# One hand-written order for all work from the last batch's outputs to the third item

## The chip, the cores and the metric

The kernel runs on one core of one Trainium2 chip. The metric is the device time of one execution in microseconds (us), lower is better, given as a median of runs. Times inside the text are positions in one profiled execution, counted from the start of its span.

## The reference

Attention without softmax feeds a router that sends each of 4608 tokens to one of 8 experts; a gated layer follows.

```python
kv = np.einsum('bhsd,bhse->bhde', k, v)            # 8 batches, 8 heads, 576 rows, width 64
out = np.einsum('bhsd,bhde->bhse', q, kv)
rms = np.sqrt(np.mean(out * out, axis=-1, keepdims=True) + 1e-06)
x = out / rms * g_norm                              # -> 4608 tokens of width 512
logits = x @ w_gate + modality_bias[modality_id]
e_idx = np.argmax(logits, axis=1)                   # one expert of 8 for each token
gate_w = softmax(logits)[arange, e_idx]
for e in range(8):
    mask = e_idx == e
    h = np.maximum(x[mask] @ w1[e], 0.0)            # 512 -> 1024
    out[mask] = gate_w[mask, None] * (h @ w2[e])    # 1024 -> 512
out = (sigmoid(out @ moe2_w_gate) * (out @ moe2_w_val)) @ moe2_w_out
```

## The kernel before

The program has three stages: attention by batch, the experts by item, and the gated layer. An item is a pair of 128-token tiles of one expert. `gather` (L200) fetches a tile's rows out of the DRAM tensor `x_d` by an indirect DMA that POOL issues; `norm_x` (L230, DVE) scales it; `emit_A` (L238) transposes it on PE and splits it into a high part `xh` (ACT) and a rest `xl` (DVE). An item has four steps, j = 0 to 3. In each step `emit_B` (L251) runs 24 matmuls with a block of w1, `emit_h` (L270) takes the relu, and `emit_D` (L305) runs 12 matmuls with a block of w2, or 8 full float32 ones where `plain` says so (odd j of items 0 and 1). `split_w` (L214) splits a block of weights on ACT (`w1h`, `w2h`) and DVE (`w1l`, `w2l`).

The first two items are formed from the first four batches alone, so that their matmuls can run while the router still counts the other tokens. The third item, t = 2, needs the finished router: after the last batch's outputs (`emit_out`, L489, with a copy and a square on ACT and a reduce on DVE) come `norm`, `choose`, `rank`, `lanes`, `numbers`, then `totals`, `segments`, `slots` and `tokens`, which end in the row list `gidx`, and `experts`, which ends in the list of experts `est`. `store_x` (L588) writes a batch to `x_d`, one DMA of 1152 KB and, for odd batches, two of 144 KB. The gather of item 2 reads any row of `x_d`, so it comes after the store of batch 7 as well.

The order is the order of emission: `manual_schedule` keeps each engine's instructions, and the DMAs that it issues, in the order of the Python code. SP issues all weight loads (`load_w`, L185) and all stores of `x_d`. Items 0, 1 and 2 share one weight buffer, `half`: each block is loaded for the next item once its last reader is done, so that SP waits at such a load for a `split_w` on DVE, or for a plain `emit_D` on PE. `read_item` (L163) makes SP read `est` into registers, and SP waits there for DVE. Loads for item 2 carry a condition (`cond=new`): where item 2 has the expert of item 1, the DMA is issued and nothing is moved.

Before, all of this is in two loops. The loop over batches (L661) has one extra round, b = 8, for the outputs of batch 7; the loop over the eight steps of items 0 and 1 (L847) hangs the router's pieces on the steps by a table:

```python
CHAIN = {0: [ranks2, norm_last], 1: [lanes2, lambda: choose(3)], 2: [number(2, 0), ranks], 3: [number(2, 1), totals, lanes3, segments, number(3, 0)],
         4: [slots, number(3, 1)], 5: [tokens], 6: [experts], 7: [places]}
```

In what follows the names are those of the change's list: `out3`, `o3`, `sq3`, `ssq3` are the matmuls, copy, square and reduce of row group 3 of batch 7; `n7b` is the end of `norm(7)`; `nx21`, `A21`, `xh21`, `xl21` belong to tile 1 of item 2; `w1h6`, `w1l6`, `B6`, `h6`, `hl6`, `w2h6`, `w2l6`, `D6` belong to step 6 (item 1, j = 2), and B8 is the first step of item 2; `L2_3` loads w2's block 3 for item 1; `S7` stores batch 7; `exp` is `experts` and the two `read_item` calls; `g0` and `g1` are gathers for items 2 and 3.

Of the kernel before, what the change touches and what calls it, by code (L numbers as in the profile page):

```python
# [35 lines left out]
NFRONT = 2  # L36
# [48 lines left out]
def attention_moe_glu_kernel(  # L85
# [76 lines left out]

    def read_item(t):  # L163
# [36 lines left out]
    def gather(t):  # L200
        if t >= al.end:
            return
        for i in range(tiles_of(t)):
# [10 lines left out]
    def split_w(t, j, which):  # L214
# [10 lines left out]
        hi, lo = al.w2() if which else [w1p.tile(shape, F32R, tag=nm + z, name=nm + z, bufs=3) for z in "hl"]  # L225
        nc.scalar.activation(out=hi, in_=src, func=ACTF.Copy)
        nc.vector.tensor_tensor(out=lo, in0=src, in1=hi, op=ALU.subtract)  # L227
        dst[t, j] = (hi, lo)
# [9 lines left out]
    def emit_A(t, i):  # L238
# [6 lines left out]
        if i == 0:  # L245
            xT_t[t] = [xp.tile([128, KC, 256], F32R, tag=z, name=z) for z in ("xh", "xl")]
        hi, lo = (z[:, :, i * 128:i * 128 + 128] for z in xT_t[t])
        nc.scalar.activation(out=hi, in_=ps, func=ACTF.Copy, scale=gcol)  # L248
        nc.vector.scalar_tensor_tensor(out=lo, in0=ps, scalar=gcol, in1=hi.bitcast(F32), op0=ALU.mult, op1=ALU.subtract)  # L249
# [20 lines left out]
    def emit_h(t, j):  # L270
# [13 lines left out]
        nc.scalar.activation(out=hi[:, :, 0:n], in_=ph, func=ACTF.Relu)  # L284
        nc.vector.scalar_tensor_tensor(out=lo[:, :, 0:n], in0=ph, scalar=0.0, in1=hi[:, :, 0:n].bitcast(F32), op0=ALU.max, op1=ALU.subtract)
# [53 lines left out]
    with ExitStack() as st:  # L339
# [149 lines left out]
        def emit_out(b, r):  # L489
# [6 lines left out]
            for hp in range(4):  # L496
                for lo, n, c in ([(0, 128, b)] if r < 4 else [(0, 64, b - 1), (64, 64, b)]):
                    nc.tensor.matmul(out=ps[lo:lo + n, hp // 2, (hp % 2) * 144:(hp % 2) * 144 + 144],
                                     lhsT=qt[:, hp, lo:lo + n], rhs=Rs[c % 3][:, hp, :], start=True, stop=True)
            nc.scalar.activation(out=o[:, r, :].rearrange("p (a f) -> p a f", a=2), in_=ps[:, :, 0:288], func=ACTF.Copy)  # L500
            sq = wk.tile([128, H, D], F32, tag="sq", name="sq")
            sqv, ov = sq.rearrange("p (c s) d -> p c (s d)", s=2), o[:, r, :].rearrange("p (c f) -> p c f", c=4)[:, :, 0:128]
            nc.scalar.activation(out=sqv, in_=ov, func=ACTF.Square)
            nc.vector.tensor_reduce(out=ssq[:, 8 * t:8 * t + 8], in_=sq, op=ALU.add, axis=AX)

        def norm(b):

# [5 lines left out]
            nc.vector.tensor_scalar(out=ms, in0=ms, scalar1=1.0 / D, scalar2=1e-6, op0=ALU.mult, op1=ALU.add)  # L513
            nc.scalar.activation(out=rt[:, v], in_=ms, func=ACTF.Sqrt)
            nc.vector.reciprocal(out=rs, in_=rt[:, v])
# [26 lines left out]

        def rank(bp):

            t0, n = 9 * bp, 9
            og = oh[:, t0:t0 + n, :]
            tr = sm.tile([128, 8], F32, tag="tr", name="tr")
            nc.vector.tensor_reduce(out=tr, in_=og.rearrange("p t e -> p e t"), op=ALU.add, axis=AX)
            nc.vector.tensor_tensor(out=tot[:, bp + 1, :], in0=tot[:, bp, :], in1=tr, op=ALU.add)
# [3 lines left out]
            for i in range(1, n):  # L553
                nc.tensor.matmul(out=ps[:, i:n, :], lhsT=onesb, rhs=og[:, 0:n - i, :], start=False, stop=(i == n - 1))
            me = me_t.pop(bp)
# [4 lines left out]
            lane = sm.tile([128, 9], BF16, tag="lane", name="lane")  # L560
# [962 lines left out]
```

## Time and profile before

| | us |
|---|---|
| median of 3 runs | 1483.66 |
| lowest and highest | 1482.23, 1486.6 |
| the profiled execution | 1486.05 |
| its span | 1484.3 |
| PE busy in the span | 1433.2 (97%) |
| the changed stretch, `out0` to B8 | 131.73 to 203.80 |

A row of a timeline gives the start, the time an instruction took, engine, line, operation, what it writes and reads, and in brackets the idle time of the engine before it with what ended it. A row of the windows gives, for a stretch, its length, each engine's busy time and number of instructions, then the clock that TensorE was granted (1.00 is 2.4 GHz, 0.50 is 1.2 GHz, a value between is a mean over the stretch), the share of the DMA engines that was busy and GB/s.

### The profile page before, as it was taken

How to read it: one execution, taken by the hardware profiler on the slowest of the kernel's cores; microseconds unless marked ns; L12 is line 12 of the kernel's file. 1: busy time of each engine (PE TensorE's matmuls, PEld its weight loads, DVE VectorE, ACT ScalarE, POOL GpSimd, SP SyncE). 2: the span in 40 equal slices, each digit the busy share in tenths (PEclk: the TensorE clock that was granted, in tenths of full speed). 3: DMA queues.
4: the chain of work that ended last, by engine and by line, in shares of the span. 5: the costliest groups of instructions: out<-in, count | busy, mean ns of one | idle time of the engine just before them, and what ended most of it. 6: DMA issues, size and time to landing. Idle time of an engine off the chain costs nothing.

```text
span 1484.3 us, 22966 instructions
## 1 busy us (share of the span) xinstructions
PE 1433.2 (97%) x8654; PEld 1223.9 (82%) x8654; DVE 902.5 (61%) x1418; ACT 639.0 (43%) x1019; POOL 218.5 (15%) x302
## 2 busy tenths in 40 slices
PE   6988899999999999999999999999999999999997
PEld 6977678999999998778888888888888888888886
DVE  2557767888888888647876676343653436444342
ACT  3656645555555555746433342232322323221221
POOL 1011021212222122311011101010010200101001
PEclk9999999999999999999999999999999999999999
DMA  9976469989896856959886666556474564646444
GB/s 297 335 289 239 180 226 282 314 289 300 289 296 207 256 182 224 307 204 351 323 333 250 245 234 237 211 199 248 156 261 188 216 231 171 247 165 235 179 156 166
DMA packets 161954, 360.49 MB, mean 243 GB/s; under 512 B 20912, under 2 KB 80560, under 8 KB 154672
## 3 DMA queue, kind: packets, MB, share of 16 engines
q1 hardware_dynamic: 149904, 325.42, 63.7%
q0 software_dynamic: 10432, 32.08, 5.9%
q8 instruction: 70, 1.15, 0.3%
q10 hardware_dynamic: 1504, 1.48, 0.3%
q14 instruction: 44, 0.36, 0.1%
HBM read 302.88 MB, written 68.63 MB: 250 GB/s over the span
## 4 chain that ended last, share of the span: by engine, by line
PE 54%; DMA 4%; SPq 0%; issue 0%; DVE 0%; ACT 0%; POOL 0%; POOLq 0%; ACTq 0%
PE gv L986 10%; PE gv L988 10%; PE gv L987 10%; PE ac L1354 6%; PE ac L1352 6%; PE ac L1353 6%; DMA xg<-x_d,gidx 3%; PE gv L962 1%; PE gv L960 1%; PE gv L961 1%; PE tr L923 1%; DMA rows<-w_d 1%; DMA half<-in_moe_w_dram 0%; DMA y_d<-y,sidx 0%; SPq L1075 0%
## 5 line engine op out<-in xcount | busy, mean ns | idle before, releaser
L990 DVE TENSOR_TENSOR gm<-u,gv 128x512 f32<-128x512 f32 x96 | 65.8, 685 | 172.5 <-PE gv L988 171.3
L265 PE MATMUL ph<-xh,w1h 128*128 128x256 f32 x576 | 167.8, 291 | 2.7 <-ACT xh L248 1.7
L1354 PE MATMUL ac<-wos,gl 128*128 128x512 f32 x432 | 168.3, 389 | 0.0
L1352 PE MATMUL ac<-wos,gh 128*128 128x512 f32 x432 | 168.2, 389 | 0.0
L1353 PE MATMUL ac<-wos,gh 128*128 128x512 f32 x432 | 168.1, 389 | 0.0
L266 PE MATMUL ph<-xh,w1l 128*128 128x256 f32 x576 | 164.6, 286 | 2.7 <-DVE w1l L227 2.7
L267 PE MATMUL ph<-xl,w1h 128*128 128x256 f32 x576 | 164.5, 286 | 0.6 <-DVE xl L249 0.6
L1010 ACT ACTIVATE s<-gv 128x512 f32<-128x512 f32 x48 | 28.7, 597 | 262.4 <-issue 205.7
L265 PEld LDWEIGHTS ph<-xh,w1h 128*128 128x128 f32 x576 | 111.5, 194 | 5.7 <-ACT xh L248 2.2
L266 PEld LDWEIGHTS ph<-xh,w1l 128*128 128x128 f32 x576 | 111.6, 194 | 4.7 <-DVE w1l L227 3.3
L986 PE MATMUL gv<-half,wt 128*128 128x512 f32 x288 | 112.9, 392 | 0.7 <-DVE u L990 0.7
L267 PEld LDWEIGHTS ph<-xl,w1h 128*128 128x128 f32 x576 | 111.7, 194 | 1.0 <-DVE xl L249 1.0
L988 PE MATMUL gv<-half,wt 128*128 128x512 f32 x288 | 112.2, 390 | 0.0
L987 PE MATMUL gv<-half,wt 128*128 128x512 f32 x288 | 112.1, 389 | 0.0
L317 PE MATMUL py<-w2h,hh 128*128 128x512 f32 x272 | 106.7, 392 | 0.0
L318 PE MATMUL py<-w2l,hh 128*128 128x512 f32 x272 | 106.7, 392 | 0.0
L319 PE MATMUL py<-w2h,hl 128*128 128x512 f32 x272 | 105.9, 389 | 0.0
L990 DVE TENSOR_TENSOR s<-u,gv 128x512 f32<-128x512 f32 x48 | 33.0, 688 | 118.6 <-PE gv L988 118.5
L1336 POOL DMA_INDIRECT out_dram<-ot,to x36 | 37.0, 1027 | 435.2 <-DVE ot L1333 187.3
L1354 PEld LDWEIGHTS ac<-wos,gl 128*128 128x128 f32 x432 | 81.1, 188 | 17.3 <-DVE gl L1321 0.4
L1352 PEld LDWEIGHTS ac<-wos,gh 128*128 128x128 f32 x432 | 81.1, 188 | 16.9 <-ACT gh L1320 0.2
L1353 PEld LDWEIGHTS ac<-wos,gh 128*128 128x128 f32 x432 | 81.1, 188 | 16.9
(309 smaller groups left out, 3341.0 us busy)
## 6 DMA issues: line engine op xcount, KB each, us to landing
wt<-wt_d SPq DMA_DIRECT2D x36, 1536.0 KB
half<-in_moe_w_dram SPq DMA_DIRECT2D x96, 512.0 KB
wos<-wo_d SPq DMA_DIRECT2D x96, 512.0 KB
w1r<-in_moe_w_dram SPq DMA_DIRECT2D x40, 512.0 KB
w2r<-in_moe_w_dram SPq DMA_DIRECT2D x40, 512.0 KB
rows<-w_d SPq DMA_DIRECT2D x24, 512.0 KB
wt<-wt_d SPq DMA_DIRECT2D x48, 256.0 KB
wt_d<-wt SPq DMA_DIRECT2D x12, 1024.0 KB
```

The costliest lines, as they stand in the source:

```text
L265: nc.tensor.matmul(out=o, lhsT=bh[:, c, cs], rhs=hi[:, c, 0:n], start=(c == 0), stop=False)
L266: nc.tensor.matmul(out=o, lhsT=bl[:, c, cs], rhs=hi[:, c, 0:n], start=False, stop=False)
L267: nc.tensor.matmul(out=o, lhsT=bh[:, c, cs], rhs=lo[:, c, 0:n], start=False, stop=(c == KC - 1))
L317: nc.tensor.matmul(out=o, lhsT=hi[:, f, cs], rhs=bh[:, f, :], start=first, stop=False)
L318: nc.tensor.matmul(out=o, lhsT=hi[:, f, cs], rhs=bl[:, f, :], start=False, stop=False)
L319: nc.tensor.matmul(out=o, lhsT=lo[:, f, cs], rhs=bh[:, f, :], start=False, stop=last)
L986: nc.tensor.matmul(out=o, lhsT=wh, rhs=yh[:, c, :], start=first and c == 0, stop=False, skip_group_check=True)
L987: nc.tensor.matmul(out=o, lhsT=wh, rhs=yl[:, c, :], start=False, stop=False, skip_group_check=True)
L988: nc.tensor.matmul(out=o, lhsT=wl, rhs=yh[:, c, :], start=False, stop=last and c == 1, skip_group_check=True)
L1352: nc.tensor.matmul(out=o, lhsT=gh[:, cs], rhs=wh, start=(k == 0), stop=False)
L1353: nc.tensor.matmul(out=o, lhsT=gh[:, cs], rhs=wl, start=False, stop=False)
L1354: nc.tensor.matmul(out=o, lhsT=gl[:, cs], rhs=wh, start=False, stop=(k == NJ - 1))
```

## The change

`emit_out`, `norm`, `rank`, `totals`, `segments`, `tokens`, `places`, `split_w`, `emit_A` and `emit_h` become generators that stop between their parts on different engines. The rest of the code calls them through `whole`, which runs all parts at once. The extra round of the batch loop, the table and the loop over steps go; a list of some 190 names takes their place and is run from left to right. A load for item 2 is emitted after the first name behind `exp` at which its block's last reader has been emitted. The amount of computation stays, with one piece on another engine.

```diff
+        def whole(parts):
+            for _ in parts:
+                pass
...
-        for b in range(B + 1):
+        for b in range(B):
...
-                if b > 2 and b % 2 == 0:
-                    if r == 0 and early or r == 1 and b == 4:
-                        lane = rank(b // 2 - 2)
-                    elif r == 1 and early or r == 3 and b == 4:
-                        lo = lanes(b // 2 - 2, lane)
...
+                if (b, r) in ((4, 1), (5, 4)):
+                    rank(b - 4)
+                if (b, r) in ((4, 3), (6, 0)):
+                    lanes(b // 2 - 2)
...
+                if early and r == 1:
+                    numbers(1, nc.scalar, (0,))
+                    numbers(1, nc.vector, (1,))
...
-        for s, (t, j) in enumerate(steps):
-            emit_B(t, j)
-            emit_h(t, j)
...
+            if t == 0:
+                for w in range(2):
+                    todo[f"L{w + 1}_{j}"] = lambda j=j, w=w: load_w(1, j, w)
...
+        place(ch3=lambda: choose(3), slots=slots, plx=exps, y0=lambda: emit_y(0), y1=lambda: emit_y(1),
+              g0=lambda: gather(NFRONT, (0,)), g1=lambda: (gather(NFRONT, (1,)), gather(NFRONT + 1)),
+              exp=lambda: (experts(), read_item(NFRONT), read_item(NFRONT + 1)))
+        behind = [(f"w1l{NJ1 + j}", j, 0) for j in range(NJ1)] + [(("D" if plain(1, j) else "w2l") + str(NJ1 + j), j, 1) for j in range(NJ1)]
+        ORDER = """
+            w1h1 out0 nx01 out1 w2h0 w1h2 o1 nx00 A00 xh00 nx10 A01 n6a w2l0 o0 xl00 nx11 out2 xh01 w1h0 xl01 out3 w1l0 rk2p o3
+            sq0 rk2 n6s o2 A11 xh11 B0 L2_0 A10 w2h2 w1l1 w1l2 sq1 ssq0 w1h3 ssq1 h0 S5 ln2 out4 sq2 hl0 o4 B1 ssq2 L1_0 w1l3 sq3
+            L1_2 h1 w1h4 B2 sq4 D0 xh10 h2 L1_1 n6b nu2b S6 xl11 xl10 nu2a B3 w2l2 ssq4 ssq3 D1 w1l4 n7a n7s hl2 B4 n7b w2h4 w1h5
+            w1h6 ch3 h4 w1l5 rk3p w1l6 rk3 D2 w2l4 ln3 h3 L1_3 nu3a B5 hl4 totp D3 tot sega segb slots soh B6 D4 exp nu3b php w1h7
+            plx gidx w1l7 h5 plc L2_2 h6 L2_1 D5 L2_3 w2h6 B7 w2l6 S7 g0 hl6 g1 nx20 A20 D6 h7 pld w1h8 nx21 xh20 A21 xl20 w1l8
+            xh21 D7 xl21 y0 y1
+        """.split()
+        done = set()
+        al.end = NSURE
+        for name in ORDER:
+            todo[name]()
+            done.add(name)
+            if "exp" in done:
+                for job in [x for x in behind if x[0] in done]:
+                    load_w(NFRONT, *job[1:])
+                    behind.remove(job)
```

The queue of SP before, from the store of batch 7 to the read of `est`; `half` rows are weight loads, the last three of them w2's blocks 2, 1 and 3 for item 1:

```order
L590 DMA x_d<-o 128x2304 [waits DMAHW2_49,Pool_49]
L594 DMA x_d<-o 64x576 [waits DMAHW3_49]
L594 DMA x_d<-o 64x576 [waits DMAHW4_49]
...
L189 DMA half_1812<-in_moe_w_dram 128x2x512 [waits DMAHW7_49,DVE_49]
L189 DMA half_1812<-in_moe_w_dram 128x2x512 [waits DMAHW0_49,PE_49]
L189 DMA half_1812<-in_moe_w_dram 128x2x512 [waits DMAHW1_49,PE_49]
L169 TENSOR_LOAD est [waits DVE_49]
```

The same queue now, from the read of `est` to the store of batch 7; between the two stand five loads for item 2, then w2's blocks 2 and 1 for item 1, block 1 for item 2 (it waits for D5 on PE), block 3 for item 1 and block 2 for item 2 (it waits for `w2l6` on DVE):

```order
L173 TENSOR_LOAD est [waits DVE_49]
...
L193 DMA half_1804<-in_moe_w_dram 128x2x512
L193 DMA half_1804<-in_moe_w_dram 128x2x512 [waits DMAHW2_49,PE_49]
L193 DMA half_1804<-in_moe_w_dram 128x2x512 [waits DMAHW2_49,PE_49]
L193 DMA half_1804<-in_moe_w_dram 128x2x512 [waits DMAHW4_49]
L193 DMA half_1804<-in_moe_w_dram 128x2x512 [waits DMAHW5_49,DMAHW1_49,DVE_49]
L623 DMA x_d<-o 128x2304 [waits DMAHW6_49,Pool_49]
L627 DMA x_d<-o 64x576 [waits DMAHW7_49]
```

Three loads for item 1 and the store of batch 7 have moved from ahead of the read of `est` to behind it, and the store also behind a load that waits for D5.

PE before, from D5 (`py<-half,hf`) by B7 (`ph`) and D6 (`py<-w,...`) to the transposes of item 2 (`xtp`):

```order
L315 MATMUL py<-half_1812,hf 128x512 x4
L265 MATMUL ph<-xh,w1h 128x256
L266 MATMUL ph<-xh,w1l 128x256
L267 MATMUL ph<-xl,w1h 128x256
...
L317 MATMUL py<-w_2512,hh 128x512
L318 MATMUL py<-w_2512,hh 128x512
L319 MATMUL py<-w_2512,hl 128x512
...
L244 MATMUL xtp<-ident,xg 128x128 x4
L315 MATMUL py<-half_1812,hf 128x512 x4
L244 MATMUL xtp<-ident,xg 128x128 x4
```

PE now, from D5 again:

```order
L332 MATMUL py<-half_1804,hf 128x512 x4
L278 MATMUL ph<-xh,w1h 128x256
L279 MATMUL ph<-xh,w1l 128x256
L280 MATMUL ph<-xl,w1h 128x256
...
L255 MATMUL xtp<-ident,xg 128x128 x4
L334 MATMUL py<-w_2548,hh 128x512
L335 MATMUL py<-w_2548,hh 128x512
L336 MATMUL py<-w_2548,hl 128x512
...
L255 MATMUL xtp<-ident,xg 128x128 x4
L332 MATMUL py<-half_1804,hf 128x512 x4
```

The two transposes of item 2 have each moved ahead by one `emit_D`: A20 stands ahead of D6, and A21 ahead of D7.

## Rows read from the trace of the kernel before

**Rows 1.** The page: busy time and share by engine; below, PE's busy tenths by slice.

```profile
PE 1433.2 (97%) x8654; PEld 1223.9 (82%) x8654; DVE 902.5 (61%) x1418; ACT 639.0 (43%) x1019; POOL 218.5 (15%) x302
PE   6988899999999999999999999999999999999997
```

**Rows 2.** Windows: busy time by engine, granted clock, DMA share, GB/s.

```profile
131.70:203.80 72.10, 62.57 (x445) 49.51 (x445) 53.33 (x137) 40.15 (x80) 6.66 (x11) 0.98 0.58 206
154.00:158.00 4.00, 4.00 (x24) 4.00 (x23) 3.10 (x8) 0.00 (x0) 0.00 (x0) 0.61 1.01 387
204.00:209.00 5.00, 4.72 (x26) 4.51 (x26) 1.76 (x2) 1.67 (x3) 3.31 (x5) 0.66 1.01 294
```

**Rows 3.** Timeline of PE, the batch loop and the end of the stretch.

```profile
90.27 3.53 PE L461 MATMUL kv<-vt,kt 64*64 64x64 f32 x113
111.75 0.17 PE L604 MATMUL tote<-tot,onesb 128*128 128x8 bf16 x1 [3.67 <-ACT qT L486]
152.46 0.63 PE L244 MATMUL xtp<-ident,xg 128*128 128x128 f32 x4 [2.61 <-issue]
187.59 3.60 PE L315 MATMUL py<-half,hf 128*128 128x512 f32 x8
193.89 0.40 PE L317 MATMUL py<-w,hh 128*128 128x512 f32 x1
196.65 0.60 PE L244 MATMUL xtp<-ident,xg 128*128 128x128 f32 x4
202.37 0.66 PE L244 MATMUL xtp<-ident,xg 128*128 128x128 f32 x4 [1.69 <-DVE xg L236]
203.80 0.39 PE L265 MATMUL ph<-xh,w1h 128*128 128x256 f32 x1 [0.78 <-ACT xh L248]
```

**Rows 4.** Timeline of ACT and DVE in the batch loop.

```profile
92.91 0.23 DVE L541 TENSOR_TENSOR oh<-me,ct 128x72 bf16<-128x72 f32 x1
111.59 2.72 ACT L584 ACTIVATE lid<-lo,ct 128x128 bf16<-128x128 bf16 x9
```

**Rows 5.** Windows and timeline of DVE in the stretch.

```profile
133.20:193.40 60.20, 53.16 (x403) 43.12 (x403) 45.95 (x115) 34.45 (x72) 6.66 (x11) 0.97 0.64 228
189.36 1.23 DVE L227 TENSOR_TENSOR w1l<-half,w1h 128x1024 fp32r<-128x1024 f32 x1 [0.25 <-ACT w1h L226]
193.22 0.18 DVE L810 CAST est<-esf 1x53 int32<-1x53 f32 x1
```

**Rows 6.** Timeline of SP's queue: when each DMA was issued.

```profile
151.14 0.32 SPq L590 DMA_DIRECT2D x_d<-o  x1
174.54 0.37 SPq L189 DMA_DIRECT2D half<-in_moe_w_dram  x1
196.09 4.69 SPq L189 DMA_DIRECT2D half<-in_moe_w_dram  x8
201.07 2.40 SPq L189 DMA_DIRECT2D w1r<-in_moe_w_dram  x4
```

**Rows 7.** Waits of SP's queue, 150 to 205 us: engine, line, for what, us, times, longest.

```profile
SPq L169 <- DVE est L810: 18.5, 1, 18.5
SPq L189 <- PE py L315: 12.8, 2, 11.1
```

**Rows 8.** DMA issues, 185 to 195 us, and windows of DMA traffic.

```profile
xg<-x_d,gidx POOLq DMA_INDIRECT x4, 4.0
125.00:136.00 11.00, 9.19 (x78) 8.98 (x77) 8.28 (x22) 9.21 (x16) 4.25 (x5) 1.00 1.00 351
141.00:158.40 17.40, 13.69 (x91) 12.07 (x91) 14.64 (x39) 4.63 (x9) 0.59 (x3) 0.90 1.02 404
198.00:200.00 2.00, 2.00 (x6) 0.89 (x5) 1.90 (x9) 1.62 (x3) 0.00 (x0) 1.00 0.00 0
201.00:202.00 1.00, 0.00 (x0) 0.00 (x0) 0.93 (x5) 0.00 (x0) 0.00 (x0) 1.00 0.00 0
202.00:203.00 1.00, 0.63 (x4) 0.42 (x4) 0.97 (x2) 0.00 (x0) 0.00 (x0) 1.00 0.65 139
```

More of the change, by code (lines that the diff above doesn't have):

```diff
@@ L198, in attention_moe_glu_kernel, with gather @@
     xg_t, xT_t, hT_t, w2s, py_t = {}, {}, {}, {}, {}
-    def gather(t):
+    def gather(t, tiles=(0, 1)):
         if t >= al.end:
             return
-        for i in range(tiles_of(t)):
+        for i in tiles[:tiles_of(t)]:
             k = first_slot(t) + i
@@ L554, in rank @@
                 nc.tensor.matmul(out=ps[:, i:n, :], lhsT=onesb, rhs=og[:, 0:n - i, :], start=False, stop=(i == n - 1))
+            yield
+            tr = sm.tile([128, 8], F32, tag="tr", name="tr")
+            nc.vector.tensor_reduce(out=tr, in_=og.rearrange("p t e -> p e t"), op=ALU.add, axis=AX)
+            nc.vector.tensor_tensor(out=tot[:, bp + 1, :], in0=tot[:, bp, :], in1=tr, op=ALU.add)
             me = me_t.pop(bp)
@@ L787, in tokens @@
         def tokens():
-            ph = [pq.tile([128, 512], F32, tag="q", name="php") for _ in range(2)]
             for t0 in range(0, NTILE, 9):
@@ L885, in attention_moe_glu_kernel, with steps, place @@
-        emit_D(*steps[-1])
-        load_w(NFRONT, NJ1 - 1, 1)
-        emit_A(NFRONT, 1)
-        emit_y(NFRONT - 1)
+        todo = {}
+        def steps(names, parts):
+            for name in names.split():
+                todo[name] = lambda: next(parts, None)
+        def place(**do):
+            todo.update(do)
+        for r in range(5):
+            steps(f"out{r} o{r} sq{r} ssq{r}", out_parts(B - 1, r))
+        for t in range(NFRONT + 1):
+            for i in range(2):
+                todo[f"nx{t}{i}"] = lambda t=t, i=i: norm_x(t, i)
+                steps(f"A{t}{i} xh{t}{i} xl{t}{i}", A_parts(t, i))
@@ new lines, in attention_moe_glu_kernel, with second @@
+        for n in range(NFRONT * NJ1 + 1):
+            t, j = divmod(n, NJ1)
+            steps(f"w1h{n} w1l{n}", split_parts(t, j, 0))
+            steps(f"w2h{n} w2l{n}", split_parts(t, j, 1))
+            steps(f"h{n} hl{n}", h_parts(t, j))
+            todo[f"B{n}"] = lambda t=t, j=j: emit_B(t, j)
+            def second(t=t, j=j):
+                if plain(t, j):
+                    w2s[t, j] = (part(t, j, 1), None)
+                emit_D(t, j)
+            todo[f"D{n}"] = second
+            if t == 0:
+                for w in range(2):
+                    todo[f"L{w + 1}_{j}"] = lambda j=j, w=w: load_w(1, j, w)
@@ new lines, in attention_moe_glu_kernel @@
+        for b in (B - 2, B - 1):
+            steps(f"n{b}a n{b}s n{b}b", norm_parts(b))
+        for b in range(B - 3, B):
+            todo[f"S{b}"] = lambda b=b: store_x(b)
+        for bp in (2, 3):
+            steps(f"rk{bp}p rk{bp}", rank_parts(bp))
+            todo[f"ln{bp}"] = lambda bp=bp: lanes(bp)
+            for w in range(2):
+                todo[f"nu{bp}{'ab'[w]}"] = lambda bp=bp, w=w: numbers(bp, nc.scalar, (w,))
+        steps("totp tot", totals())
+        steps("sega segb", segments())
```

143 lines of the change are left out of this document (51 added, 92 removed).

## The prediction

> **What bounds the kernel now.** I read the page first: PE is busy for 1433.2 of 1484.3 us, and its slices are full but for the first seven, one in the middle and the last [rows 1]. So what the stretch before the third item loses on PE is lost at the end, and what it gains is gained there; behind B8 PE stays full, and I carry a shift of B8 through at its full size. Then the windows: from `out0` at 131.73 to B8 at 203.80 PE works for 62.57 of 72.10 us [rows 2, 3]. It idles for 9.5 us, and it loses a little more where the clock was granted at the lower of its two levels: the mean is 0.61 over 154 to 158, after an idle time of 2.61 us ahead of a transpose, and 0.66 over 204 to 209, after the waits for A21 and B8 [rows 2, 3]. At 0.66 those 5 us do the work of 3.3, so 1.7 us are lost; by the 4 us at 0.61, another 1.6. All that an ideal order of this stretch could win is thus 9.5 + 1.7 + 1.6 = 12.8 us, and some 2 us more in the batch loop (below).
>
> Next SP's queue, since the change moves rows there. Before, SP waits 11.1 us for a plain `emit_D` (D3) ahead of `L2_3`, and then 18.5 us for `est` [rows 7]. Everything that items 0 and 1 need is out by 174.54, and the store of batch 7 was issued at 151.14, 35 us ahead of the gather that reads it [rows 6]. So no wait of SP touches PE before. `est` is done at 193.22 + 0.18 = 193.40 [rows 5]; the first of eight loads behind it goes out at 196.09, so reading the registers takes 2.7 us, and the last of them waits for D7. No data follows these eight (0 GB/s over 198 to 200, [rows 8]): item 2 has item 1's expert in these inputs, so its loads cost SP issue time alone. Eight took 4.69 us with the wait for D7 among them, and one alone 0.37 [rows 6]; I take 0.43 each.
>
> **The change part by part.** *The batch loop.* Half of `numbers(1)` goes from ACT (the 2.72 us at 111.59, [rows 4]) to DVE. PE waited 3.67 us for ACT there [rows 3]; DVE's pieces that wait for ACT come earlier. Against it, `rank(1)` now stands ahead of the key-value matmuls of batch 6, which began at 90.27 [rows 3]; it needs `choose(1)`, whose last piece ends at 92.91 + 0.23 = 93.14 [rows 4], so PE waits 2.9 us there. Part of that is eaten by the later wait, since the rank's pieces leave the path in front of `numbers`. I take a gain of 2 us at `out0`; the ends are a gain of 3.5 and a loss of 1.
>
> *The stretch up to `est`.* In the new order DVE does nearly all of its old work before `est`, and it is DVE that sets `est`. From `nx00` at about 133.3 to `est` DVE was busy for 45.95 of 60.2 us [rows 5]; of the rest, mostly waits for other engines, I take 1.8 us as gaps inside its chains, which stay. Four pieces now come behind `est`: `w1l7` and `w2l6` (1.2 each by the row at 189.36), `hl6` and the three of `gidx` (0.7 and 0.6), and one `nx` (0.7), 4.4 in all. That leaves 43.4 us. DVE starts at 133.3 - 2 = 131.3, so `est` can't be done before 174.7. Two waits are added. ACT has `w1h2` ahead of `o1` and `o0`; its block is the fifth load. Five loads (2.6 MB) and four gathers (1.2 MB) take some 10.8 us at 351 GB/s from 125 on [rows 8], so ACT stands until about 136 - 2 = 134. `xl00` then costs DVE 2.1 us, and `out2`, which needs `o0`, costs PE 3.5; two matmul groups later `rk2` waits for PE for another 2.1. With 1 us at `totp`, `est` is done at about 174.7 + 5.3 = 180, 13 us ahead of before. PE has reached the end of `php` at about 181.3: it had no other long wait on the way, and most of the old ones (2.61 ahead of `xtp`, [rows 3]) are gone.
>
> *D5.* It is here that SP's new order is felt. `L2_2` and `L2_1` stand behind `est`, the register reads (2.7) and five loads for item 2 (5 x 0.43 = 2.1). `L2_2` is issued at 180 + 4.8 = 184.8, `L2_1` at 185.3. Data begins some 1.2 us after an issue (the DMA of 201.07, nothing to 202, 139 GB/s from there, [rows 6, 8]), and 1.05 MB take 2.6 us at the best rate of 404 GB/s, somewhat longer for a queue that starts empty. So `L2_1` lands at about 189, and D5, which reads it, waits from 181.3 to 189.0: **7.7 us of idle PE**. D5 itself is 3.5 us (3.60 with its tail, [rows 3]), and after so long a wait at the lower clock about 1.7 more: it ends at 194.5.
>
> *A20.* Behind `L2_1` SP has the load of block 1 for item 2, which may not overwrite what D5 reads: SP stands until 194.5. Then: that load 0.43, `L2_3` 0.37, the next load 0.43, and only then `S7`, issued at 195.7. `L2_3` and the store move 0.5 + 1.5 MB, 5 us at 404 GB/s [rows 8], and data begins 1.2 us after the first issue: `S7` has landed at about 201.8. POOL's gather waits for it; a gather takes 4.0 us from issue to landing [rows 8], `nx20` 0.7. A20 starts at 206.5. PE finished B7 (2.8 us, from 191.1 to 193.89 before, [rows 3]) at 197.3, and A20 stands ahead of D6 and D7, so PE has nothing to do: **9.2 us of idle PE**. This wait doesn't depend on when `est` comes: from the end of D5 to A20 it is 1.2 + 6.1 + 4.0 + 0.7 = 12 us, against 2.8 of B7.
>
> *From A20 to B8.* A20 0.43, D6 2.76 (193.89 to 196.65), A21 0.43, D7 3.5, and 1.7 for the lower clock: B8 starts at 206.5 + 8.8 = 215.3, with `xl21` 216.
>
> *Sum.* B8 comes at 216 instead of 203.8, 12.2 later. Of that 1.7 is given back, since before paid the lower clock of 204 to 209 behind B8; `y0` and `y1`, now side by side on ACT ahead of the next split, cost 0.4. That makes +11 us. The profiled execution took 1486.05; it would be 1497. The median is 2.4 below it, 1483.66, so I forecast **1494.7 us**.
>
> *Moved at no cost.* The generators add no instruction; `exps` (with its table load), `slots` and `places` run beside PE. `y0`'s store to `y_d` moves behind `y1`'s, and no one reads it before the last stage.
>
> **A rule against this order.** Before, `S7` was issued at 151.14 and the gather of item 2 found it landed [rows 6]. The Trainium skill (DMA: Bandwidth & Descriptors, Rules for kernel authors) says the same as advice: issue a DMA early, compute, and wait for its semaphore late. The change does the reverse with the store and three loads. With the store issued as soon as `n7b` allows, at about 161, the 9.2 us and the clock behind them would go and the sum would be near 0; by the queue as it stands it is +11. The trace of before agrees with the rule; that the reverse costs what I say no run here has shown yet.
>
> **The rivals.** (1) *No change.* The gather is held by several semaphores, and the rows of the order don't say which count of each; if it doesn't stand behind `S7`'s landing, A20 comes with `gidx` and the second idle time vanishes. Then 11 - 9.2 - 1.7 = 0: 1484. For it: no trace shows a gather waiting for a store. Against it: the gather may read any row of `x_d`, and its list of waits names the three lanes that `S7` uses. (2) *Faster.* The same, and DVE reaches `est` so early that `L2_1` is there when PE comes to D5. That is so if `est` is done 7.7 us before my 180, at 172, which is under my bound of 174.7; or if PE reaches D5 late for other reasons, which wins nothing. Its mechanism would be that the parts of the chain interleave with fewer gaps and the gains of the batch loop are larger. Time: 1484 - 7.7 - 1.7 = 1475. If all PE waits went, it would be 1483.7 - 12.8 - 2 = 1469. The point from which it decides is whether A20 waits less than 1 us. (3) *Slower than forecast.* The 2.9 us ahead of `rank(1)` are not eaten but kept, with the 2 us of gain gone: 1494.7 + 4 = 1499; with a D5 that waits 3 us longer, because `est` comes late, 1502. (4) *Slower, but less.* `est` at its bound of 174.7 takes 5.3 us from the wait for D5: 1489.4.
>
> **How the numbers follow.** About 0.3%, 4.5 us, is what a measurement of this kernel can tell from no change. My forecast with rivals 3 and 4 holds 0.81: forecast 0.5, rival 3 0.16, rival 4 0.15. Rival 1 has 0.11 and rival 2 0.08. Rival 4's 1489.4 is slower by over 0.3% (the bound is 1488.1), but close to it; I leave 0.02 of it within. So slower 0.79, same 0.13, faster 0.08. The range leaves out rival 2 and the better part of rival 1, and above it the sum of both mishaps: 1485 to 1502.
>
> **What would show it.** In the new trace D5 should wait 5 to 10 us with a load of `half` as its releaser, and A20 7 to 11 us behind `nx20`, the gather, and `S7`; SP's queue should show a store of `x_d` alone, some 40 us behind the other three, right after a wait for PE. B8 should start at 212 to 219. PE should wait about 3 us ahead of `rank(1)`'s matmuls and hardly at all for ACT 20 us later. The step on SP is wrong if the last store is out before `gidx`; the step on DVE is wrong if `est` is done before 175 or after 186; the carrying through is wrong if B8 moves by a size other than the end does.

## The result, and the profile after

The changed kernel takes 1500.86 us (median of 6 runs, 1496.28 to 1501.51) against 1484.41 us of the kernel before in the same comparison: a ratio of 1.0102, 95% interval 1.0084 to 1.0120. It is slower, by some 15 us. The profiled execution took 1500.97 us with a span of 1499.2 us; before, these were 1486.05 and 1484.3. So the two traces differ by 14.9 us, about what the medians differ by. One caution for all that follows: a trace is one execution, and the executions of one of these kernels lie up to 10 us apart, so positions are compared across several traces wherever a few microseconds matter.

The page of the changed kernel, busy time of PE and its slices (before: [rows 1]):

```profile
PE 1436.4 (96%) x8654; PEld 1227.4 (82%) x8654; DVE 903.6 (60%) x1419; ACT 635.3 (42%) x1010; POOL 218.0 (15%) x302
PE   6988768999999999999999999999999999999997
```

The slices of 37.5 us say where to look: the fifth falls from 8 tenths to 7 and the sixth from 9 to 6, and the seventh, 225 to 262 us, when B8 is long done, from 9 to 8. The timeline of PE in the changed kernel, the rows that answer to [rows 3] (start, duration, engine, line; in brackets the idle time ahead and what ended it):

```profile
91.16 0.21 PE L581 MATMUL rkp<-oh,ubf 128*128 128x72 bf16 x1 [2.86 <-DVE oh L569]
107.22 0.17 PE L637 MATMUL tote<-tot,onesb 128*128 128x8 bf16 x1 [2.54 <-ACT qT L503]
127.84 2.20 PE L518 MATMUL ops<-R,qT 128*128 128x144 f32 x16 [1.47 <-DVE R L496]
173.29 1.98 PE L812 MATMUL php<-soh,lid 128*128 128x44 bf16 x72
183.58 5.55 PE L332 MATMUL py<-half,hf 128*128 128x512 f32 x8 [8.31 <-DMA half<-in_moe_w_dram]
202.95 1.11 PE L255 MATMUL xtp<-ident,xg 128*128 128x128 f32 x4 [10.95 <-DVE xg L244]
211.95 0.68 PE L278 MATMUL ph<-xh,w1h 128*128 128x256 f32 x1
221.91 0.36 PE L278 MATMUL ph<-xh,w1h 128*128 128x256 f32 x1
255.09 0.39 PE L278 MATMUL ph<-xh,w1h 128*128 128x256 f32 x1 [3.52 <-ACT w1h L234]
256.93 0.58 PE L279 MATMUL ph<-xh,w1l 128*128 128x256 f32 x1 [1.45 <-DVE w1l L236]
```

`out0` starts at 127.84 (131.73 before), D5 at 183.58 after 8.31 us of waiting, A20 at 202.95 after 10.95, B8 at 211.95 (203.80 before). The row at 221.91 is the first matmul of B10, the third B of item 2; there the clock is full in both kernels, so it is the better mark. In the kernel before it is at 214.83. That splits the 14.9 us: **7.1 us are lost up to B10, and 7.8 us behind it**, where 1499.2 - 221.91 = 1277.3 us remain against 1484.3 - 214.83 = 1269.5. The last two rows are the loss behind it: TensorE stands for ScalarE's split of `w1` while item 3 is being computed.

Windows of the changed kernel (length, busy time of PE, PEld, DVE, ACT and POOL with counts, granted clock, DMA share, GB/s); the first answers to the first of [rows 2]:

```profile
127.84:211.95 84.11, 63.52 (x446) 50.91 (x446) 53.02 (x137) 39.68 (x80) 5.62 (x9) 0.86 0.43 152
128.00:173.50 45.50, 44.17 (x321) 37.58 (x321) 42.52 (x113) 33.15 (x69) 0.43 (x2) 1.00 0.52 186
178.00:182.00 4.00, 0.00 (x0) 0.00 (x0) 0.00 (x0) 0.00 (x0) 0.00 (x0) 0.50 0.54 197
198.00:202.00 4.00, 0.00 (x0) 0.00 (x0) 0.00 (x0) 0.00 (x0) 2.76 (x3) 0.50 0.36 88
236.00:244.00 8.00, 8.00 (x51) 7.17 (x51) 4.51 (x6) 5.24 (x7) 2.20 (x2) 1.00 0.63 44
254.00:258.00 4.00, 1.46 (x6) 1.26 (x7) 3.81 (x6) 3.99 (x6) 0.60 (x2) 0.71 1.07 389
258.00:262.00 4.00, 4.00 (x21) 4.00 (x21) 3.69 (x5) 0.00 (x0) 0.00 (x0) 0.50 1.05 378
```

From `out0` to B8 PE idles 20.6 us, 9.5 before. Up to `php` the new order is excellent: 44.17 of 45.50 us busy at full clock. Then come the two holes, each with the clock at its lower level behind it. The window of 236 to 244 belongs to the loss behind B8: the DMA engines move 44 GB/s for 8 us, though SyncE issues four loads of 512 KB from 234.99 to 242.82.

SyncE's queue in the changed kernel (start of the issue, duration from the first to the last of a group), to be read beside [rows 6]; then the first gather on GpSimd, `est` and `nx20` on VectorE:

```profile
146.20 0.34 SPq L623 DMA_DIRECT2D x_d<-o  x1
146.91 43.46 SPq L193 DMA_DIRECT2D half<-in_moe_w_dram  x11
190.48 0.35 SPq L623 DMA_DIRECT2D x_d<-o  x1
212.92 2.52 SPq L193 DMA_DIRECT2D w1r<-in_moe_w_dram  x4
242.99 0.82 SPq L127 DMA_DIRECT2D d_raw<-in_moe_w_gate_dram  x1
...
198.62 0.97 POOL L211 DMA_INDIRECT xg<-x_d,gidx  x1 [43.88 <-DMA x_d<-o]
...
173.45 0.18 DVE L828 CAST est<-esf 1x53 int32<-1x53 f32 x1
202.21 0.69 DVE L244 TENSOR_TENSOR xg<-xg 128x512 f32<-128x512 f32 x1 [17.10 <-DMA xg<-x_d,gidx]
```

The store of the last batch, 151.14 before, goes out at 190.48. `gidx` is done at 176.0, but the gather starts only at 198.62, released by that store; its data and `nx20` come ahead of A20. `est`, the thing that the order was arranged around, is done 20 us earlier than before, and TensorE gains nothing by it: the load that it waits for next stands behind `est` on SyncE.

### The profile page after: what moved, and what is told of

The parts are those of the page before. It is cut to its first block, busy times and chain, and to the rows that moved or that the text cites. A ratio compares the mean times of both kernels' runs of the same rounds, so it can differ in the third digit from the quotient of the medians.

```text
span 1499.2 us, 22942 instructions
## 1 busy us (share of the span) xinstructions
PE 1436.4 (96%) x8654; PEld 1227.4 (82%) x8654; DVE 903.6 (60%) x1419; ACT 635.3 (42%) x1010; POOL 218.0 (15%) x302
## 4 chain that ended last, share of the span: by engine, by line
PE 53%; DMA 4%; issue 1%; POOL 1%; DVE 0%; ACT 0%; POOLq 0%; ACTq 0%
PE gv L1011 10%; PE gv L1013 10%; PE gv L1012 10%; PE ac L1379 6%; PE ac L1377 6%; PE ac L1378 6%; DMA y_d<-y,sidx 3%; PE gv L986 1%; PE gv L985 1%; PE gv L987 1%; PE tr L948 1%; POOL gate_t L939 0%; DMA gate_t<-gate_d,oid 0%; DMA d_raw<-y_d 0%; POOL xg L211 0%
```

## The experiments

My theory was that three losses stand side by side and have one cause, DMAs issued late on SyncE's in-order queue: item 1's loads behind `est` (D5), the store behind those loads (A20), and item 3's loads behind D7 (the wait at 255). The rivals: the gather waits for something else; the waits cover for one another, so that removing one lengthens the next; the loss behind B8 has nothing to do with when item 3's loads start. Ratios are to the kernel before, run on the same chip.

### Each late DMA by itself, and both

**e1_store_early.** The store back to where its data allows it.

```
-  ... D2 w2l4 ln3 h3 L1_3 nu3a B5 ...        ... w2h6 B7 w2l6 S7 g0 ...
+  ... D2 w2l4 ln3 h3 L1_3 S7 nu3a B5 ...     ... w2h6 B7 w2l6 g0 ...
```

> The changed kernel with one name moved: the store of the last batch, S7, now stands right behind the load L1_3, ahead of the register reads of est and of item 2's loads; nothing else moves. Theory (the first gather waits for this store to land): the 10.95 us that the transpose A20 waits behind D5 go, to under 2 us, the half clock that follows them goes too, the first gather starts at about 176 us when gidx is set, and B8 comes some 11 to 14 us earlier than at 212.4 us. D5 still waits about 8 us for its half load. Time 1487 us if about 6 us are still lost behind B8, 1481 to 1484 if that loss goes with the rest. Rival (the gather waits for something else that comes late, and the store only happens to end there): A20 stays near 203 us, the time stays within 3 us of 1501.

1490.1 us, ratio 1.0032 (1.0016 to 1.0048). SyncE issues the store at 153.14, the first gather starts with `gidx`, and `nx20` no longer waits; A20 and A21 run without a wait, and B8 is at 199.19, 12.8 us earlier than in the changed kernel. The rival falls. D5 still waits, 10.1 us. The time is 3 us above the 1487 that I had expected with a loss left behind B8; the trace is that of the fastest of the ten executions (1486.06).

```profile
174.99 1.23 POOL L211 DMA_INDIRECT xg<-x_d,gidx  x1 [21.88 <-DVE gidx L817]
183.34 0.68 DVE L244 TENSOR_TENSOR xg<-xg 128x512 f32<-128x512 f32 x1
183.56 6.23 PE L332 MATMUL py<-half,hf 128*128 128x512 f32 x8 [10.06 <-DMA half<-in_moe_w_dram]
```

**e2_loads_early.** The three loads ahead of the register reads, the store left late.

```
-  ... w2l2 ssq4 ssq3 D1 w1l4 ... totp D3 tot ... plc L2_2 h6 L2_1 D5 L2_3 w2h6 ...
+  ... w2l2 L2_2 ssq4 ssq3 D1 L2_1 w1l4 ... totp D3 L2_3 tot ... plc h6 D5 w2h6 ...
```

> The changed kernel with the three second-weight loads of item 1 (L2_2, L2_1, L2_3) moved ahead of the register reads of est: L2_2 behind w2l2, L2_1 behind D1, L2_3 behind D3. S7 stays late. Theory: the 8.3 us that D5 waits for its half load go with the lower clock behind them; S7 still follows a load that waits for D5, so A20's wait stays at 9 to 12 us, all of it 8 to 10 us earlier; B8 at 203 to 205 us, time 1491 to 1493 us. Rival (item 2's loads, first in the queue anyway, or the late est set when D5 can run): D5 still stands over 4 us, the time moves by under 4 us.

1486.48 us, ratio 1.0006 (0.9990 to 1.0023). D5 runs on behind `php` with no wait at full clock; A20 still waits, 8.3 us, for the gather that waits for the store. B8 is at 196.55, earlier than the 203 to 205 that I had expected, and the time some 5 us better: I had not counted D5's own slow clock (5.55 us, now 3.68), A20's wait is 2.6 us shorter, and `php` is 1.9 us earlier in this execution.

```profile
173.18 3.68 PE L332 MATMUL py<-half,hf 128*128 128x512 f32 x8
183.72 0.97 POOL L211 DMA_INDIRECT xg<-x_d,gidx  x1 [31.12 <-DMA x_d<-o]
188.04 1.11 PE L255 MATMUL xtp<-ident,xg 128*128 128x128 f32 x4 [8.32 <-DVE xg L244]
```

**e3_both_early.** Both edits together.

> The changed kernel with both moves: S7 behind L1_3, and L2_2, L2_1, L2_3 behind w2l2, D1, D3. Theory (the two waits are apart and add up): both go, B8 at 188 to 193 us against 203.8 us in the kernel before, and what is left of the loss depends on item 3's loads, which still start when D7 ends, right ahead of B8: 1476 us if about 6 us are lost behind B8 as in the changed kernel, 1470 us if nothing is. Rival (the waits cover for one another: with one gone the other grows, or the loads and the store share the DMA engines): the gain over the changed kernel is under 16 us, that is a time of 1485 us or more.

1477.15 us, ratio 0.9954 (0.9937 to 0.9971): faster than the kernel before. In units of the ratio the store alone gives back 0.0070, the loads alone 0.0096, both 0.0148 of 0.0166 if they simply added up. So the two waits are apart, and the rival that they cover for one another falls. B8 comes at 189.47, and TensorE still waits 3.7 and 1.3 us behind it, as in the changed kernel: 1475.6 - 199.42 = 1276.2 us remain from B10 on.

### The loss behind B8

**e4_d7_ahead.** TensorE gets D6 and D7 ahead of A20; the list is otherwise that of the changed kernel.

```
-  ... nx20 A20 D6 h7 pld w1h8 nx21 xh20 A21 xl20 w1l8 xh21 D7 xl21 y0 y1
+  ... nx20 D6 h7 D7 A20 pld w1h8 nx21 xh20 A21 xl20 w1l8 xh21 xl21 y0 y1
```

> The changed kernel with D6, h7 and D7 moved ahead of the transpose A20 on TensorE's queue; S7 and all loads keep their place in the list, but the load that waits for D7 and item 3's loads behind it can start as soon as D7 ends, some 10 us before B8 instead of with it. Theory (A20's wait is for the store, and the 6 us lost behind B8 are item 3's loads that start too late): A20's wait falls from 11 to 3 to 6 us since D6 and D7 fill the rest, B8 at 204 to 208 us, the PE wait near 251 us falls from 3.5 us to under 2 and its half clock goes: 1487 to 1490 us. Rival (the loss behind B8 doesn't depend on when item 3's loads start): B8 earlier by the same 5 to 8 us, the time 1493 to 1496 us.

1492.39 us, ratio 1.0049 (1.0032 to 1.0067). Half of it went as expected: with D7 done early, item 3's loads start at 201.07, 11.6 us ahead of B8, and behind B8 nothing is lost (PE 20.00 of 20.00 us busy from 240 to 260, clock 1.00). The other half didn't: A20 still waits 7.0 us and A21 2.0, B8 starts at 212.67, no earlier than in the changed kernel (its `est` is 2.8 us later in this execution, and its gathers run beside the loads). The gain is all behind B8.

**e6_item3_first.** From here on the base is e3_both_early. One load changes its place on SyncE: item 2's last, which waits for D7, goes behind item 3's eight.

```
     behind = [...] + [(("D" if plain(1, j) else "w2l") + str(NJ1 + j), j, 1)
-                      for j in range(NJ1)]
+                      for j in range(NJ1 - 1)]
...
     load_w(lo + 1, j, which)          # item 3, in run()
+    load_w(lo, NJ1 - 1, 1)            # behind the two loops over item 3's loads
```

> The kernel e3_both_early with one load moved on SyncE: item 2's last load, the one that waits for D7 to free its place, now stands behind item 3's eight loads, so these no longer wait for D7. TensorE's order is as in e3_both_early. Theory (the loss near 232 us, 3.7 and 1.3 us of waits and 6 us at half clock, is item 3's loads that start 1 us behind B8): they are issued 4 to 10 us ahead of B8, as early as the memory that they go to is free, the waits on w1h and w1l at 228 to 236 us fall under 1.5 us and the clock stays full; time 1470 to 1473 us. Rival (memory that D7 or something later still reads holds them, or the order of the loads alone doesn't matter since the DMA engines are full): the wait stays, 1476 to 1478 us.

1468.12 us, ratio 0.9911 (0.9898 to 0.9924): the fastest of all, 1% under the kernel before, and better than I expected. Item 3's loads start at 179.51, 9.2 us ahead of B8 (188.74). ScalarE's timeline shows what they do, first in the changed kernel, then in this one (with a window of this kernel behind it, where TensorE is full at full clock):

```profile
245.54 0.69 ACT L260 ACTIVATE xh<-xtp,gcol 128x512 fp32r<-128x512 f32 x1 [1.64 <-PE xtp L255]
253.43 0.66 ACT L133 ACTIVATE d_e<-d_raw 128x512 f32<-128x512 f32 x1 [7.20 <-DMA w1r<-in_moe_w_dram]
253.99 1.04 ACT L234 ACTIVATE w1h<-w1r 128x1024 fp32r<-128x1024 f32 x1
```

```profile
222.33 0.69 ACT L260 ACTIVATE xh<-xtp,gcol 128x512 fp32r<-128x512 f32 x1 [1.64 <-PE xtp L255]
222.92 0.66 ACT L133 ACTIVATE d_e<-d_raw 128x512 f32<-128x512 f32 x1
223.49 1.04 ACT L234 ACTIVATE w1h<-w1r 128x1024 fp32r<-128x1024 f32 x1
240.00:260.00 20.00, 20.00 (x137) 18.41 (x136) 17.73 (x24) 11.20 (x15) 5.95 (x6) 1.00 0.99 335
```

The wait is not for item 3's weights. ScalarE stands at `d_e`, the first step of decoding another weight; it reads `d_raw`, which was loaded behind item 3's and more, and the split that TensorE needs (`w1h`) is next in ScalarE's queue. (The profile names a load of `w1r` as the releaser in the changed kernel and `d_raw` itself in e3_both_early. By the times at which the traces have the semaphores of `d_e` set, it is `d_raw` in both: its load lands at 253.36 in the first and at 231.07 in the second, 0.1 us ahead of `d_e`.) All that follows item 3's loads on SyncE moves with them, `d_raw` too.

**e7_three.** e3_both_early with e4's order of TensorE.

> The kernel e3_both_early with D6, h7 and D7 ahead of the transpose A20, as in e4_d7_ahead. Theory: D7 ends 3 to 4 us earlier and item 3's loads with it, but A20, A21 and the split of their result now stand uncovered in front of B8, which costs 1.5 to 3 us there; the loss of 6 us behind B8 falls to 1 to 2 us: 1472 to 1475 us. Rival (the uncovered chain in front of B8 and the clock behind it cost as much as is gained): 1476 to 1479 us.

1476.2 us, ratio 0.9963 (0.9949 to 0.9976), no different from e3_both_early: the rival held. The wait behind B8 falls only to 1.7 and 1.5 us, as item 3's loads start 1.4 us ahead of B8, and A20 and A21 stand uncovered in front of it.

**e8_after_item3_first.** The edit of e6 alone, on the changed kernel.

> The changed kernel itself with only the load of e6_item3_first moved: item 2's last load behind item 3's eight loads; the store S7 and item 1's loads stay late. Theory: D5 waits 8 us and A20 9 to 13 us as in the changed kernel (the loads now share the DMA engines with the store and the gather, which can add 1 to 3 us), the loss of 6 us behind B8 goes: 1495 to 1498 us against 1500.9. Rival (the loss behind B8 isn't from the start of item 3's loads): 1500 to 1503 us.

1495.24 us, ratio 1.0091 (1.0076 to 1.0106); the interval overlaps that of the changed kernel, so the time alone doesn't settle the gain. The trace tells both halves apart: behind B10 1492.7 - 225.79 = 1266.9 us remain, 10.4 less, and B10 itself is 3.9 later, since the gathers now share the DMA engines with item 3's loads (A20 waits 13.6 us).

**e9_before_item3_first.** The same edit on the kernel before.

> The kernel before, with only the load of e6_item3_first moved: item 2's last load stands behind item 3's eight loads. Theory (behind B8 the stretch from the second B of item 2 to the end of the span is 1276 us where item 3's loads start 1 us after B8, 1269.5 in the kernel before, where they start 2.7 us ahead of it, and 1267 where they start 9 us or more ahead): the loads start some 4 to 8 us earlier, the 1.9 us idle of TensorE near 246 us goes, and the time falls by 1.5 to 3 us, to a ratio of 0.998 to 0.999. Rival (the kernel before loses nothing to these loads, the 2 us are from something else): ratio within 0.001 of 1.

1482.15 us, ratio 0.9992 (0.9980 to 1.0005): the time doesn't decide. In the trace TensorE has no wait behind B8, and 1267.1 us remain behind B10 instead of 1269.5. (The expectation calls B10 the second B of item 2; it is the third.)

All twelve kernels and the two given ones on one table, by the lead of item 3's first load over B8:

| kernel | w1r issued | B8 | lead | ScalarE idle at `d_e` | from B10 to the end |
|---|---|---|---|---|---|
| changed | 212.92 | 211.95 | -1.0 | 7.20 | 1277.3 |
| e1, e2, e3, e5 | | | -1.0 | 7.4 to 8.5 | 1275.2 to 1276.2 |
| e7 | 187.89 | 189.28 | 1.4 | 5.42 | 1270.8 |
| before | 201.07 | 203.80 | 2.7 | 4.11 | 1269.5 |
| e9 | 198.29 | 203.14 | 4.9 | 0 | 1267.1 |
| e6 | 179.51 | 188.74 | 9.2 | 0 | 1267.4 |
| e10 | 181.09 | 190.53 | 9.4 | 0 | 1267.2 |
| e4, e8 | | | 11.6, 20.4 | 0 | 1266.7, 1266.9 |
| e11 | 191.14 | 190.18 | -1.0 | 10.98 | 1280.2 |
| e12 | 180.81 | 189.93 | 9.1 | 8.40 | 1275.4 |

In all rows but the last two the loss goes with the lead, to within 2 us (1275.2 to 1277.3 at a lead of -1.0), and it is gone at 5 us of lead. The kernels of the table differ in other edits too; e6, e8 and e9 each change the place of that one load against their base, and nothing else.

**e11_gate_late and e12_item3_gate_late.** What makes the load of `d_raw` so late? Between it and item 3's loads stand four small stores of the gates. The same edit on e3_both_early (e11) and e6_item3_first (e12):

```
-                if not s and sure:
+                if s == 6 and sure:
                     store_gate()
```

> The kernel e3_both_early with the four stores of the gates (gate_d) and the three VectorE steps ahead of them moved six steps later, behind the first load of the weights that are decoded (d_raw). Item 3's loads start 1 us behind B8 as before. Theory (the loss of 9 us behind B8 needs both: loads that start late, and the stretch of some 10 us at 54 to 175 GB/s that the gate stores put between them and d_raw): d_raw lands 5 to 8 us earlier, ScalarE no longer stands at d_e with the split of w1 behind it, the wait of 3.7 us and the half clock go, the stretch from B10 to the end falls from 1276 to 1267 to 1270 us, time 1468 to 1472 us. Rival (the late start of the loads alone makes the loss, or the stores do the same harm six steps later): 1475 to 1478 us.

> The kernel e6_item3_first with the gate stores moved six steps later as in e11_gate_late. Theory (with item 3's loads early nothing waits for them any more, so the stores cost nothing where they are): within 1.5 us of 1468.1. Rival (the stores still delay something in e6_item3_first): 1464 to 1466 us; other rival (later they delay loads that have less time to spare): 1470 us or more.

e11: 1479.88 us, ratio 0.9967 (0.9953 to 0.9982), no gain over e3_both_early. e12: 1477.3 us, ratio 0.9954 (0.9935 to 0.9973), 6 us (by the ratios) to 9 us (by the medians) slower than e6_item3_first. The first `d_e` no longer waits, the first half of the theory: its load goes out at 212.92, ahead of the stores. But the second `d_e` waits, with a store as the releaser (timeline of ScalarE in e11, and of SyncE):

```profile
224.36 0.66 ACT L133 ACTIVATE d_e<-d_raw 128x512 f32<-128x512 f32 x1
245.23 0.66 ACT L133 ACTIVATE d_e<-d_raw 128x512 f32<-128x512 f32 x1 [10.98 <-DMA gate_d<-gate]
...
212.92 0.58 SPq L127 DMA_DIRECT2D d_raw<-in_moe_w_gate_dram  x1
219.60 0.35 SPq L127 DMA_DIRECT2D d_raw<-in_moe_w_gate_dram  x1
...
232.82 1.35 SPq L1084 DMA_DIRECT2D gate_d<-gate  x1
234.21 1.91 SPq L127 DMA_DIRECT2D d_raw<-in_moe_w_gate_dram  x1
```

This second wait is a different one. The `d_e` at 245.23 reads the load of 219.60, which was issued 11 us ahead of the stores. What it waits for is its own buffer: the tile `gate`, which the stores read, and `d_e` share a single one.

```python
self.e = self.pool.tile([128, 512], F32, tag="d_e", name="d_e", bufs=1)
...
gate = dec.tile([128, 512], F32, tag="d_e", name="gate", bufs=1)[:, 0:NTILE]
```

Where the stores stood, the first `d_e` was due when they had landed (at 223.8 and 221.5 in e3_both_early); six steps later one is due 1.4 us after the last of them is issued, and it stands until that one has landed, at 245.12 in e11. So the edit took one wait away and put another in, and the times of e11 and e12 say nothing about whether the theory has the right cause; that e12 lies in the range of its second rival, 1470 us or more, is not for the rival's reason. What the pair does show is the first `d_e`: with the late loads and the stores ahead of `d_raw` it waits (7.4 us in e3), with early loads and the stores where they were it doesn't (e6), and with the late loads and the stores out of the way it doesn't either (e11). The loss behind B8 takes both. What late loads would cost at the end with no stores in the way is not shown, since e11 pays for the buffer.

### The batch loop

**e5_rank_back.** e3_both_early with `rank(1)`, its lanes and both halves of its numbers back in their old places.

```
-                if (b, r) in ((4, 1), (5, 4)):
-                    rank(b - 4)
-                if (b, r) in ((4, 3), (6, 0)):
+                if (b, r) in ((4, 1), (6, 0)):
+                    rank(b // 2 - 2)
+                if (b, r) in ((4, 3), (6, 1)):
...
-                    numbers(1, nc.vector, (1,))
+                if early and r == 2:
+                    numbers(1, nc.scalar, (1,))
```

> The kernel e3_both_early with the batch-loop part of the change undone: rank(1), its lanes and its numbers stand at batch 6 again (first, second, and second and third output), both halves of the numbers on ScalarE. Theory (the change in the batch loop gains what the first matmul of out0 showed, 131.73 us before and 127.84 after, and that gain is carried to the end): TensorE's 2.9 us wait ahead of rank(1) goes, out0 starts 3 to 5 us later than in e3_both_early, and the time is 2 to 4 us longer than its 1477.15: 1479 to 1481 us. Rival (the clock in that stretch, which is below full for much of 90 to 126 us, or a wait behind out0 takes the gain back): within 1 us of 1477.

1481.36 us, ratio 0.9992 (0.9982 to 1.0002); the intervals of the two don't overlap. By the medians 4.2 us, by the ratios some 5.6: the batch-loop part of the change gains that much, and it reaches the end. `out0` starts 2.6 us later than in e3_both_early (130.10 against 127.55), less than the 3 to 5 that I had expected, so the trace puts only part of it there. The wait ahead of `rank(1)` (2.9 us) goes, the one for ScalarE grows from 2.5 to 3.7 us, and a wait of 3.1 us comes inside the key-value matmuls of batch 6. The kernel before has that wait too, and the changed kernel has not:

```profile
96.61 1.97 PE L461 MATMUL kv<-vt,kt 64*64 64x64 f32 x31 [2.81 <-issue]
```

**e10_numbers_back.** e6_item3_first with only the second half of the numbers back on ScalarE.

> The kernel e6_item3_first with one piece of the batch-loop part undone: the second half of numbers(1) on ScalarE at the third output of batch 6, as in the kernel before; rank(1) and its lanes keep their new, earlier place. It tells which piece made the 4 us by which e5_rank_back is slower than e3_both_early. Theory (the earlier rank, with its 2.9 us wait ahead of it, gains little; what gains is ScalarE's share of numbers that VectorE takes): time 3 to 5 us over 1468.1, that is 1471 to 1473. Rival (the early place of rank gains by itself): within 1.5 us of 1468.1.

1470.82 us, ratio 0.9924 (0.9909 to 0.9938): 2.7 us slower by the medians, 1.9 by the ratios (the two ran on different chips), with overlapping intervals. That lies between the theory's 3 to 5 and the rival's 1.5. How the gain divides between the earlier rank and VectorE's half stays open.

## Why the prediction was right, and where it wasn't

Slower was right, the two waits in front of B8 came as they were worked out, and the time lies in the range, at its upper end: 1500.9 against 1494.7. That it lies there is in part luck, as the last two points show. Step by step:

- **The batch loop.** A gain of 3.9 us instead of 2, a little past the end of 3.5 that I had set. The wait of 2.86 us ahead of `rank(1)` is there as worked out, but it comes in place of another that I had overlooked: in the kernel before TensorE stood for 2.81 us inside the key-value matmuls behind it (the row of [rows 3] counts only 113 of the 144). Why it stood there the profile doesn't say, so that the one replaced the other is read from the rows and not tested.
- **`est`.** Done at 173.6, not 180. That is under the 175 that the prediction had named as the sign that its step on VectorE is wrong, and even 1 us under my bound of 174.7, which was made with a gain of 2 us in the batch loop; with the 3.9 measured it is 172.8. The terms that were mis-sized are the two added waits and the 3.5 us at `out2`. In this execution they don't come at all: ScalarE splits `w1h2` at 129.77 with no wait, so its load was there at least 4 us before the 134 that I had, and PE is busy for 44.17 of 45.50 us up to `php`. But one trace doesn't settle it. In ten traces in which VectorE's order up to there is this one, `est` starts at 171.5 to 176.3, and in seven of them ScalarE does wait for that load, for 0.6 to 2.9 us; there `est` starts 46.3 to 49.6 us after `out0`, in the other three 45.6 to 46.6. So the wait is real, at up to 2.3 us at `out2` and not 3.5, and 180 is outside. The rows of e4_d7_ahead:

```profile
132.31 1.06 ACT L234 ACTIVATE w1h<-half 128x1024 fp32r<-128x1024 f32 x1 [2.59 <-DMA half<-in_moe_w_dram]
133.96 3.41 PE L518 MATMUL ops<-R,qT 128*128 128x144 f32 x16 [2.34 <-ACT o L521]
176.29 0.18 DVE L828 CAST est<-esf 1x53 int32<-1x53 f32 x1
```

- **D5.** 8.31 us of waiting against 7.7, and 5.55 us at the lower clock against 3.5 + 1.7. The early `est` was worth nothing to this wait: PE came to D5 as much earlier as the loads did. So rival 4, which gave the early `est` back to D5, named the right event with the wrong effect; e2 shows what does take the wait away, the place of three loads.
- **A20.** 10.95 us against 9.2. SyncE issued the store 5.2 us earlier than I had it, and it then took 8.1 us, not 6.1, until the gather started. The gather itself, 3.6 us to `nx20`, and the chain are as worked out. Rival 1 is out by the gather's own row. That the wait doesn't hang on D5's wait is shown by e2: with D5's wait gone it is still 8.3 us. That it doesn't hang on `est`, as the prediction said, e2 doesn't show: there SyncE, coming from `est`, the register reads and five loads, waits only 0.4 us for D5 before it goes on to the store.
- **B8.** 211.95 against 216, that is 8.2 us later than before instead of 12.2; at B10, with the clock's price paid in both, 7.1 instead of 10.9. D5 starts 5.4 us earlier than I had it, and from D5 to B8 it takes 28.4 us, not 27. About 1 us of the 216 are slips of the sum: D5 from 189.0 with 3.5 and 1.7 us ends at 194.2, not 194.5, and the store, with data from 1.2 us after the first issue and 5 us of transfer, lands at 200.8, not 201.8.
- **Carried through at full size.** This is the step that failed, by 7.8 us, and the prediction had named its sign: B8 moved by 8.2 us and the end by 14.9. I argued from PE's full slices behind B8 in the kernel before [rows 1] (and miscounted them in front: the first, third, fourth and fifth are below 9 and the last, none in the middle). A full slice says that nothing was waited for there by then, not how much was left over: a slice of 37 us at "9" hid 1.9 us of idling near 246, and SyncE's rows showed item 3's loads starting at 201.07, 2.7 us ahead of B8 [rows 6]. In the new list D7 stands right ahead of B8, and the loads behind it start 1 us after B8. I had both rows and didn't put them side by side. The idling in the kernel before, at the same two matmuls that wait 3.52 and 1.45 us in the changed one:

```profile
244.93 0.39 PE L265 MATMUL ph<-xh,w1h 128*128 128x256 f32 x1 [0.44 <-ACT w1h L226]
246.78 0.39 PE L266 MATMUL ph<-xh,w1l 128*128 128x256 f32 x1 [1.47 <-DVE w1l L227]
```

Thus two errors of opposite sign, 3.8 us too dear in front and 7.8 us too cheap behind, left 4 us in the trace (1497 forecast for the profiled execution, 1500.97 measured). That they cancelled was luck.

**The rule that was weighed.** The prediction said that with the store issued as soon as its data allow, the sum would be near 0. e1 did just that, and it isn't 0: by the ratio its time is 0.3% above that of the kernel before, some 5 us, with 1 outside the interval. The two profiled executions, 1486.06 and 1486.05, agree by chance, since that of e1 is the fastest of its ten. In these two traces it is a difference of two terms that I didn't have: up to B10 e1 is 5.7 us ahead of the kernel before (209.14 against 214.83), and behind it it loses 5.7. The Trainium skill (DMA: Bandwidth & Descriptors, Rules for kernel authors) advises to issue a DMA early and to wait for it late. The trace of e3_both_early agrees with it at two places at once, and that of e6_item3_first at a third.

## What to carry to other kernels

An order that is good for the engines can be bad for the queue that issues their loads and stores: write down for each DMA the earliest moment that its data and its place allow, and look at what stands ahead of it in the in-order queue and waits for something else. When a step is moved, also follow what is queued behind it on that queue, one stage further than the step itself: here a load that waits for one matmul group held eight loads that didn't, and the price fell due 40 us later, on another engine. And a full slice is no proof of slack: before carrying a shift through, compare how long ahead of its use each transfer of the next stage lands, before and after. An experiment that moves a piece can bring in a wait of its own, too: look at which buffers its tiles share before reading its time.

## What the runs showed of the hardware

- Four stores of gates, two of 8 KB and two of 1 KB, cost other transfers more than their size. From 236 to 244 us in the changed kernel 44 GB/s are moved, against 385 from 224 to 228 and 380 from 250 to 254; from 228 to 246, 1726 of 4114 packets are under 512 bytes. The slow stretch moves with the stores: with the stores issued from 206.31 to 212.50 in e3 it lies at 213 to 222, and in e11, where they are issued from 230.72 to 234.17, at 237 to 246 (windows of e3, then of e11). The load of `d_raw`, 512 KB, issued behind them at 242.99 in the changed kernel, is read at 253.43. The stores themselves hold the buffer that they read until 245.23 in e11 and 242.40 in e12, 12.4 and 10.2 us after the issue of the last of them. The Trainium skill (DMA: Bandwidth & Descriptors, Specifications) gives 512 bytes as the least transfer for the full rate. The traces agree with the direction; how much of the stretch is due to the size of the packets no run here separates.

```profile
213.00:222.00 9.00, 9.00 (x58) 8.10 (x57) 4.98 (x6) 5.24 (x7) 2.19 (x2) 1.00 0.74 46
213.00:222.00 9.00, 9.00 (x60) 8.22 (x59) 4.73 (x6) 5.10 (x7) 2.19 (x2) 1.00 1.07 372
237.00:246.00 9.00, 4.02 (x23) 3.19 (x21) 0.08 (x1) 0.77 (x2) 0.00 (x0) 1.00 0.86 54
```

- The store of the last batch with its two small parts (128 x 2304 and twice 64 x 576 values of 4 bytes, 1.47 MB) is seen by the gather that waits for it 8.1 us after its issue in the changed kernel and 6.3 us in e2 (177.46 to 183.72).
- Executions of one list of instructions differ by some 5 us: the first plain `emit_D` (D1) starts at 149.84 in e1 and at 154.45 in e4, whose lists are the same up to there, and `est` at 171.5 to 176.3 over ten traces. Up to 3 us of it go with the wait for the load of `w1h2`, which is there in seven of the ten. The granted clock is below full for stretches of a few microseconds between 85 and 125 us, not at the same places: 0.68 from 90 to 95 and 0.77 from 110 to 115 in the changed kernel, 0.66 from 105 to 110 in e2, 0.57 from 95 to 100 in the kernel before. A term of 2 us there can't be read from one pair of traces.
